# Fourier mixing and a two-layer MLP on one core: PSUM banks in a fixed turn, six output buffers, and a reordered first batch

## The chip, the cores and the metric

The kernel runs on one NeuronCore of a Trainium2 chip. The metric is the device time of one execution in microseconds. The engines are PE (matrix multiply), DVE (vector), ACT (scalar), POOL (GpSimd) and SP, which here only issues transfers. The span in a profile is about 1.8 us shorter than the time of the same execution. Full clock (warm) and half clock (cold) mean a granted PE clock of 1.00 and 0.50 in the trace; in the profile of the kernel before the inverse matmuls of 512 columns follow each other by 426 to 427 ns at 0.50 (33.3 to 34.6 us) and by 215 to 217 ns at 1.00 (35.0 to 36.3 us). In this kernel PE's results go into tiles of PSUM, one or two banks each; the program has another engine evacuate a tile (copy it, or multiply it into SBUF) before PE fills the bank again, and in the profile of before PE waits 2.51 us, to 32.09 us, for DVE to have done so.

## The reference, cut to what matters

Eight batches of 3008 positions x 256 channels are filtered along the sequence (real FFT, product with a complex filter, inverse FFT). The 24064 filtered rows then pass through a two-layer MLP, 256 to 2048 to 256, with a leaky ReLU between.

```python
X = np.fft.rfft(x, axis=1)
y = np.fft.irfft(X * (filt_r + 1j * filt_i)[None], n=x.shape[1], axis=1)
h = y.reshape(B * S, D) @ w_in
out = np.maximum(0.01 * h, h) @ w_out
```

## The kernel before

The FFT is factored as 94 x 32, so all of it is matmuls: a first stage (`s1`), a transpose on DVE (`t1`), a spectral stage (`s2`), the filter products, an inverse stage (`sa`), a second transpose (`t2`) and a last stage (`sb`). Batches 1 to 7 are interleaved with the MLP of earlier rows. Batch 0 has nothing to hide behind: it is done first, in two halves of 128 channels, by routines of its own (`first_s1`, `first_s2`, `first_sa`, `first_sb`). I call everything up to the first MLP matmul the head.

The filter products of the first batch are shared out. DVE takes the chunks that begin at frequency column 0 and 16, straight from PSUM. For chunks 8 and 20 ACT copies PSUM to SBUF (`fx`) and POOL multiplies. POOL's products are put into the pool of output buffers (`outp`), which is not yet needed for output.

```python
outp = ctx.enter_context(tc.tile_pool(name="outst", bufs=4))
php = ctx.enter_context(tc.tile_pool(name="php", bufs=2, space=bass.MemoryType.PSUM))   # two banks each
pop = ctx.enter_context(tc.tile_pool(name="pop", bufs=1, space=bass.MemoryType.PSUM))
pfp = ctx.enter_context(tc.tile_pool(name="pfp", bufs=3, space=bass.MemoryType.PSUM))
...
def first_s2(hf, c, n, on_pool):
    ps = php.tile([P, n, DH], FP32, tag="ph", name=f"f2_h{hf}_c{c}")
    ...                                     # spectral matmuls into ps
    if on_pool:
        y = [outp.tile([P, n, DH], FP16, tag="ost", name=f"fy{i}_h{hf}_c{c}") for i in range(2)]
        ...                                 # act copies ps to fx; gpsimd multiplies fx into y
    else:
        ...                                 # vector multiplies ps into y
...
first_s2(0, 8, 8, True)
first_s2(0, 0, 8, False)
first_s2(0, 20, 4, True)
first_s2(0, 16, 4, False)
for g in range(8):
    first_s1(1, g, two[0], dve if g in (1, 3, 6) else act)
x_load(1)
t1_part(0, 2, True)(), t1_part(0, 3, True)()
upper(1)
first_sa(0, 0), first_sa(0, 16)
first_s2(1, 8, 8, True)
nc.gpsimd.dma_start(w_out_sb[:], moe_w_out.rearrange("(ct p) d -> p ct d", p=P))
first_s2(1, 0, 8, False)
first_s2(1, 16, 8, False)
first_sa(0, 8), first_sa(0, 20)
first_sa(1, 0)
...                                         # t2, first_sa(1, 16), first_sa(1, 8), keep_warm, first_sb
```

Of the kernel before, what the change touches and what calls it, by code (L numbers as in the profile page):

```python
# [10 lines left out]
P = 128  # L11
FP16 = mybir.dt.float16
FP32 = mybir.dt.float32
AL = mybir.AluOpType
AF = mybir.ActivationFunctionType
# [3 lines left out]
N1, N2 = 94, 32  # L19
# [46 lines left out]
def kernel(  # L66
# [9 lines left out]
    nc = tc.nc  # L76
    B, N, D = x.shape
# [5 lines left out]
    CH = 512  # L83
# [21 lines left out]
    gtp = ctx.enter_context(tc.tile_pool(name="gtp", bufs=2))  # L105
    scrp = ctx.enter_context(tc.tile_pool(name="scr", bufs=2))
    ypp = ctx.enter_context(tc.tile_pool(name="ypp", bufs=4))
    outp = ctx.enter_context(tc.tile_pool(name="outst", bufs=4))
    php = ctx.enter_context(tc.tile_pool(name="php", bufs=2, space=bass.MemoryType.PSUM))
    pop = ctx.enter_context(tc.tile_pool(name="pop", bufs=1, space=bass.MemoryType.PSUM))  # L110
    pfp = ctx.enter_context(tc.tile_pool(name="pfp", bufs=3, space=bass.MemoryType.PSUM))


    po_ps = pop.tile([P, 2, D], FP32, name="po_ps")

    ctx.enter_context(tc.manual_schedule())

# [2 lines left out]
    DH = D // 2  # L120
# [36 lines left out]

    def s1_group(b, g, copy=nc.scalar.copy):
        def go():
            ps = pfp.tile([P, 2, D], FP32, tag="pf", name=f"s1_b{b}_g{g}")  # L160
            for j in range(2):
                n2 = 2 * g + j
                nc.tensor.matmul(ps[:, j, :], f1_sb[:N1, n2, :], x_sb[:N1, n2, :],  # L163
                                 start=True, stop=True)
            spread(big[(4 * b) % 3], 2 * g, ps, copy)
        return go


    def paired(t):
        return t[:].rearrange("p (e n t) -> p n e t", n=Q, t=2)  # L170

    def spread(dst, n0, ps, copy, e0=0):
        nn, de = ps.shape[1], ps.shape[2] // 2
        copy(paired(dst)[:, ds(n0, nn), ds(e0, de)], ps[:].rearrange("p n (e t) -> p n e t", t=2))  # L174

    E4 = D // 2 // 4

# [19 lines left out]
    ys = {}  # L197

    def s2_group(b, g):
        def go():  # L200
            ps = pfp.tile([P, 2, D], FP32, tag="pf", name=f"s2_b{b}_g{g}")
            src = big[(4 * b + 1) % 3][:].rearrange("p (n d) -> p n d", n=Q)
            nc.tensor.matmul(ps[:], fwd2, src[:, ds(2 * g, 2), :], start=True, stop=True)  # L203
            fa, fb = fa_sb[:, ds(2 * g, 2), :], fb_sb[:, ds(2 * g, 2), :]
            p1 = scrp.tile([P, 2, D], FP32, tag="p1", name=f"p1_b{b}_g{g}")
            p2 = scrp.tile([P, 2, D], FP32, tag="p2", name=f"p2_b{b}_g{g}")
            nc.vector.tensor_tensor(p1[:], ps[:], fa, AL.mult)  # L207
            nc.vector.tensor_tensor(p2[0:64], ps[64:P], fb[64:P], AL.mult)  # L208
            nc.vector.tensor_tensor(p2[64:P], ps[0:64], fb[0:64], AL.mult)  # L209
            y1 = ypp.tile([P, 2, D], FP16, tag="y", name=f"y_b{b}_g{g}")  # L210
            nc.gpsimd.tensor_tensor(y1[:], p1[:], p2[:], AL.add)  # L211
            ys[(b, g)] = y1
        return go

    def sa_group(b, g):
        def go():
            ps = pfp.tile([P, 2, D], FP32, tag="pf", name=f"sa_b{b}_g{g}")
            nc.tensor.matmul(ps[:], inv2, ys.pop((b, g))[:], start=True, stop=True)  # L218
            spread(big[(4 * b + 2) % 3], 2 * g, ps, nc.scalar.copy)
        return go  # L220

    def sb_group(b, g, copy, pool=(pfp, "pf")):
        dt, h = g // 8, g % 8

        def go():
            src = big[(4 * b + 3) % 3][:].rearrange("p (h n d) -> p h n d", h=2, n=Q)
            ps = pool[0].tile([P, 4, N1], FP32, tag=pool[1], name=f"sb_b{b}_g{g}")
            for j in range(4):
                n2 = 4 * h + j
                nc.tensor.matmul(ps[:, j, :], src[:, dt, n2, :], i1_sb[:, n2, :],  # L230
                                 start=True, stop=True)
            yv = yts[b % 2][:, dt, :].rearrange("p (a c) -> p a c", c=N2)
            copy(yv[:, :, ds(4 * h, 4)], ps[:].rearrange("p c a -> p a c"))  # L233
        return go


    two = ((pfp, "pf"), (php, "ph"))
    act, dve = nc.scalar.copy, nc.vector.tensor_copy

    def first_s1(hf, g, pool, copy):  # L240
        ps = pool[0].tile([P, 4, DH], FP32, tag=pool[1], name=f"f1_h{hf}_g{g}")
        for j in range(4):
            n2 = 4 * g + j
            nc.tensor.matmul(ps[:, j, :], f1_sb[:N1, n2, :], x_sb[:N1, n2, ts(hf, DH)],  # L244
                             start=True, stop=True)
        spread(big[0], 4 * g, ps, copy, hf * DH // 2)


    def first_s2(hf, c, n, on_pool):
        ps = php.tile([P, n, DH], FP32, tag="ph", name=f"f2_h{hf}_c{c}")  # L250
        src = paired(big[1])
        for j in range(0, n, 4):
            nc.tensor.matmul(ps[:, ds(j, 4), :].rearrange("p n (e t) -> p n e t", t=2), fwd2,
                             src[:, ds(c + j, 4), ts(hf, DH // 2)], start=True, stop=True)
        fs = [f[:, ds(c, n), ts(hf, DH)] for f in (fa_sb, fb_sb)]
        if on_pool:
            y = [outp.tile([P, n, DH], FP16, tag="ost", name=f"fy{i}_h{hf}_c{c}") for i in range(2)]
            xs = [scrp.tile([P, 4, DH], FP32, tag=f"p{j // 4 + 1}", name=f"fx_h{hf}_c{c + j}")
                  for j in range(0, n, 4)]
            for j, xf in enumerate(xs):  # L260
                act(xf[:], ps[:, ts(j, 4), :])
            for i in range(2):
                for j, xf in enumerate(xs):
                    nc.gpsimd.tensor_tensor(y[i][:, ts(j, 4), :], xf[:], fs[i][:, ts(j, 4), :], AL.mult)  # L264
        else:
            y = [ypp.tile([P, n, DH], FP16, tag=f"yw{i}", bufs=2, name=f"fy{i}_h{hf}_c{c}")
                 for i in range(2)]
            for i in range(2):
                nc.vector.tensor_tensor(y[i][:], ps[:], fs[i], AL.mult)  # L269
        ys[(hf, c)] = y  # L270

    def first_sa(hf, c):
        y = ys.pop((hf, c))
        for j in range(0, y[0].shape[1], 4):
            ps = pfp.tile([P, 4, DH], FP32, tag="pf", name=f"fa_h{hf}_c{c + j}")
            for i, m in enumerate((inv2, inv2x)):
                nc.tensor.matmul(ps[:], m, y[i][:, ds(j, 4), :], start=(i == 0), stop=(i == 1))
            act(paired(big[2])[:, ds(c + j, 4), ts(hf, DH // 2)],
                ps[:].rearrange("p n (t e) -> p n e t", t=2))


    def first_t2(i):
# [1 line left out]
        o = big[0][:].bitcast(FP32).rearrange("p (h n e r) -> p h e n r", h=2, n=Q // 2, r=2)  # L284
        nc.vector.transpose(o[:, i // 2, ts(i % 2, E4)], a)

    def first_sb(g, copy, pool):
        dt, h = g // 8, g % 8
        src = big[0][:].rearrange("p (h n e r t) -> p h n r t e", h=2, n=Q // 2, r=2, t=2)
        ps = pool[0].tile([P, 4, N1], FP32, tag=pool[1], name=f"fb_g{g}")  # L290
        for j in range(4):
            n2 = 4 * h + j
            for t in range(2):
                nc.tensor.matmul(ps[64 * t : 64 * t + 64, j, :], src[:, dt, n2 // 2, n2 % 2, t, :],  # L294
                                 i1_sb[:, n2, :], start=True, stop=True)
        yv = yts[0][:, dt, :].rearrange("p (a c) -> p a c", c=N2)
        copy(yv[:, :, ds(4 * h, 4)], ps[:].rearrange("p c a -> p a c"))

    def upper(hf):
        for t, cp in ((fa_sb, act), (fb_sb, dve)):  # L300
# [2 lines left out]

    def keep_warm(n):
        for _ in range(n):
            nc.tensor.matmul(po_ps[:].rearrange("p a d -> p (a d)"), small_sb[:, 0, :],
                             i1_sb[:].rearrange("p a d -> p (a d)")[:, 0:512],
                             start=True, stop=True)

# [6 lines left out]
    first_s2(0, 20, 4, True)  # L316
    first_s2(0, 16, 4, False)
    for g in range(8):
        first_s1(1, g, two[0], dve if g in (1, 3, 6) else act)
    x_load(1)  # L320
    t1_part(0, 2, True)(), t1_part(0, 3, True)()
    upper(1)
    first_sa(0, 0), first_sa(0, 16)
    first_s2(1, 8, 8, True)
    nc.gpsimd.dma_start(w_out_sb[:], moe_w_out.rearrange("(ct p) d -> p ct d", p=P))
    first_s2(1, 0, 8, False)
    first_s2(1, 16, 8, False)
    first_sa(0, 8), first_sa(0, 20)
    first_sa(1, 0)
    first_t2(0), first_t2(1)  # L330
    first_sa(1, 16), first_sa(1, 8)
# [13 lines left out]
    def moe1_group(ci, g):  # L345
        if g == 0:
            gts[ci] = gtp.tile([P, NCT, CH], FP16, tag="gt", name=f"gt_c{ci}")
        ph = php.tile([P, 2, CH], FP32, tag="ph", name=f"h_c{ci}_g{g}")
        pieces, t = [], ci * CH
        while t < (ci + 1) * CH:  # L350
            e = min((ci + 1) * CH, (t // N + 1) * N)
            pieces.append((t // N, t % N, t - ci * CH, e - t))
            t = e
        for j in range(2):
            ct = 2 * g + j
            for b, lo, o, ln in pieces:
                for dt in range(NDT):
# [2 lines left out]
                        yts[b % 2][:, dt, ds(lo, ln)],  # L360
                        start=(dt == 0), stop=(dt == NDT - 1),
                    )
        nc.scalar.activation(gts[ci][:, ds(2 * g, 2), :], ph[:], AF.Lrelu)  # L363

    def moe2_slice(ci, g):
        tj, half = g // 2, g % 2
        last = ci == NCHUNK - 1
        if last and half == 0:
            pos[ci] = pfp.tile([P, D], FP32, tag="pf", name=f"o_c{ci}_t{tj}")[:]
        po = pos[ci] if last else po_ps[:, tj % 2, :]  # L370
        for ct in range(8 * half, 8 * half + 8):
            nc.tensor.matmul(po, gts[ci][:, ct, ts(tj, P)], w_out_sb[:, ct, :],  # L372
# [77 lines left out]
```

## Time and profile before

| | before |
|---|---|
| time, median of the first 6 runs | 787.69 us (787.64 to 789.57) |
| span of the profiled run | 786.4 us |
| PE busy | 763.3 us, 97% |
| ACT, DVE, POOL busy | 556.9, 365.0, 150.6 us |
| first MLP matmul | 46.27 us |
| from there to the end | 740.03 us |

PE is busy for 97% of the span, so little can be gained; what there is lies in the first 46 us. The prediction shows the lines. Here, before and after, one line of the list of waits matters besides. It gives what PE waited for in total, how often, and the longest single wait; this is PE's wait for the two halves of the input of the first batch:

```profile
PE f_h_g L244 <- DMA x_sb<-in_x_dram: 9.5, 2, 9.2
```

### The profile page before, as it was taken

To read this page: it belongs to the slowest core of one execution; us is meant where nothing else is said; L and a number is where in the kernel's file an instruction comes from. 1 tells how busy PE (TensorE), PEld (TensorE's weight loads), DVE (VectorE), ACT (ScalarE), POOL (GpSimd) and SP (SyncE) were. 2 spreads that over 40 slices of the span, in tenths; PEclk is the share of its full clock that TensorE was granted. 3 is DMA by queue.
4 is the path that set the end of the run, shared out by engine and by line. 5 is a ranking of instruction groups with operands and counts; after the bars stand their busy time and mean duration, and the time that the engine had idled before them with its cause. 6 is when DMAs were issued, how large, how long until landed. Compare 5 with 4: busy or idle time off the path is not lost.

```text
span 786.4 us, 13584 instructions
## 1 busy us (share of the span) xinstructions
PE 763.3 (97%) x5812; PEld 527.9 (67%) x5812; DVE 365.0 (46%) x459; ACT 556.9 (71%) x794; POOL 150.6 (19%) x122
## 2 busy tenths in 40 slices
PE   3799999999999999999999999999999999999998
PEld 2356677666776677866777667776677667676666
DVE  4768760784327652386416764078432765200000
ACT  4686768676687767877687775967668776666664
POOL 6583400240003400042001410024000340000000
PEclk9999999999999999999999999999999999999999
DMA  9953010501032010501014101050100101101111
GB/s 176 203 68 95 28 42 28 121 28 41 28 76 73 28 41 28 117 33 42 28 41 108 40 29 41 28 119 28 43 28 28 41 28 42 41 28 41 41 41 54
DMA packets 42011, 43.38 MB, mean 55 GB/s; under 512 B 14274, under 2 KB 40514, under 8 KB 41282
## 3 DMA queue, kind: packets, MB, share of 16 engines
q0 software_dynamic: 15760, 16.99, 13.1%
q1 hardware_dynamic: 26192, 25.53, 9.3%
q8 instruction: 45, 0.74, 0.4%
q14 instruction: 14, 0.11, 0.0%
HBM read 34.10 MB, written 24.64 MB: 75 GB/s over the span
## 4 chain that ended last, share of the span: by engine, by line
PE 93%; ACT 3%; DVE 2%; DMA 1%; POOL 1%; issue 1%; POOLq 0%; ACTq 0%; DVEq 0%
PE po_ps L372 41%; PE h_c_g L358 40%; PE s_b_g L163 3%; PE sb_b_g L230 2%; PE s_b_g L203 2%; PE sa_b_g L218 2%; DMA x_sb<-in_x_dram 1%; DVE fy_h_c L269 1%; PE o_c_t L372 1%; ACT big L174 1%; ACT gt_c L363 1%; PE f_h_g L244 0%; POOL fy_h_c L264 0%; PE fb_g L294 0%; ACT fa_sb L301 0%
## 5 line engine op out<-in xcount | busy, mean ns | idle before, releaser
L363 ACT ACTIVATE gt_c<-h_c_g 128x1024 f16<-128x1024 f32 x376 | 384.6, 1023 | 194.0 <-PE h_c_g L358 193.0
L358 PE MATMUL h_c_g<-yt,w_in_sb 128*128 128x512 f16 (+7 forms) x1728 | 386.6, 352 | 0.7 <-ACT gt_c L363 0.4
L372 PE MATMUL po_ps<-w_out_sb,gt_c 128*128 128x256 f16 x2944 | 381.4, 273 | 0.6 <-ACT ost_c_t L379 0.6
L372 PEld LDWEIGHTS <-gt_c 128*128 128x128 f16 x3008 | 290.3, 98 | 87.1 <-issue 1.7
L358 PEld LDWEIGHTS <-w_in_sb 128*128 128x128 f16 x1728 | 162.7, 98 | 95.7 <-issue 1.4
L211 POOL TENSOR_TENSOR y_b_g<-p_b_g,p_b_g 128x512 f16<-128x512 f32 x84 | 106.9, 1273 | 225.7 <-DVE p_b_g L209 225.7
L186 DVE STREAM_TRANSPOSE big<-big 128x1024 f32<-128x1024 f32 x32 | 55.8, 1843 | 127.3 <-ACT big L174 127.1
L233 DVE CAST yt<-sb_b_g 128x376 f16<-128x376 f32 x112 | 56.3, 545 | 85.9 <-PE sb_b_g L230 85.9
L207 DVE TENSOR_TENSOR p_b_g<-s_b_g,fa_sb 128x512 f32<-128x512 f32 x84 | 58.1, 692 | 38.8 <-PE s_b_g L203 36.0
L379 ACT COPY ost_c_t<-po_ps 128x256 f32<-128x256 f32 x184 | 69.4, 377 | 7.4 <-PE po_ps L372 6.1
L194 DVE STREAM_TRANSPOSE big<-big 128x1024 f32<-128x1024 f32 x28 | 51.1, 1933 | 34.5 <-ACT big L174 34.5
L208 DVE TENSOR_TENSOR p_b_g<-s_b_g,fb_sb 64x512 f32<-64x512 f32 x84 | 58.2, 692 | 1.1
L209 DVE TENSOR_TENSOR p_b_g<-s_b_g,fb_sb 64x512 f32<-64x512 f32 x84 | 57.4, 683 | 1.1
L125 POOL DMA_DIRECT2D x_sb<-in_x_dram x12 | 8.5, 711 | 253.6 <-PE s_b_g L163 252.5
L174 ACT CAST big<-s_b_g 128x512 f16<-128x512 f32 x104 | 57.0, 607 | 0.0
L174 ACT CAST big<-sa_b_g 128x512 f16<-128x512 f32 x84 | 50.6, 602 | 0.0
L230 PEld LDWEIGHTS <-big 128*128 128x128 f16 x448 | 25.6, 98 | 13.2
L163 PE MATMUL s_b_g<-x_sb,f_sb 94*128 94x256 f16 x224 | 33.8, 272 | 0.3
L203 PE MATMUL s_b_g<-big,small_sb 128*128 128x512 f16 x84 | 31.9, 379 | 0.0
L218 PE MATMUL sa_b_g<-y_b_g,small_sb 128*128 128x512 f16 x84 | 31.9, 379 | 0.0
L230 PE MATMUL sb_b_g<-i_sb,big 128*128 128x94 f16 x448 | 28.7, 206 | 0.0
L163 PEld LDWEIGHTS <-f_sb 94*128 94x128 f16 x224 | 21.0, 97 | 9.1 <-issue 0.6
(42 smaller groups left out, 160.4 us busy)
## 6 DMA issues: line engine op xcount, KB each, us to landing
out_dram<-ost_c_t SPq DMA_DIRECT2D x92, 256.0 KB, 2.1
x_sb<-in_x_dram POOLq DMA_DIRECT2D x6, 1536.0 KB, 10.8
x_sb<-in_x_dram POOLq DMA_DIRECT2D x4, 384.0 KB, 10.2
w_in_sb<-in_moe_w_in_dram POOLq DMA_DIRECT2D x1, 1024.0 KB, 15.8
w_out_sb<-in_moe_w_out_dram POOLq DMA_DIRECT2D x1, 1024.0 KB, 9.9
x_sb<-in_x_dram POOLq DMA_DIRECT2D x1, 1024.0 KB, 9.1
f_sb<-fwd_const SPq DMA_DIRECT2D x4, 192.0 KB, 3.2
fa_sb<-in_filt_r_dram POOLq DMA_DIRECT2D x4, 192.0 KB, 10.0
```

Source lines behind the costliest of these rows:

```text
L163: nc.tensor.matmul(ps[:, j, :], f1_sb[:N1, n2, :], x_sb[:N1, n2, :], start=True, stop=True)
L174: copy(paired(dst)[:, ds(n0, nn), ds(e0, de)], ps[:].rearrange("p n (e t) -> p n e t", t=2))
L207: nc.vector.tensor_tensor(p1[:], ps[:], fa, AL.mult)
L208: nc.vector.tensor_tensor(p2[0:64], ps[64:P], fb[64:P], AL.mult)
L209: nc.vector.tensor_tensor(p2[64:P], ps[0:64], fb[0:64], AL.mult)
L211: nc.gpsimd.tensor_tensor(y1[:], p1[:], p2[:], AL.add)
L230: nc.tensor.matmul(ps[:, j, :], src[:, dt, n2, :], i1_sb[:, n2, :], start=True, stop=True)
L233: copy(yv[:, :, ds(4 * h, 4)], ps[:].rearrange("p c a -> p a c"))
L358: nc.tensor.matmul(ph[:, j, ds(o, ln)], w_in_sb[:, dt, ts(ct, P)], yts[b % 2][:, dt, ds(lo, ln)], start=(dt == 0), stop=(dt == NDT - 1),)
L363: nc.scalar.activation(gts[ci][:, ds(2 * g, 2), :], ph[:], AF.Lrelu)
L372: nc.tensor.matmul(po, gts[ci][:, ct, ts(tj, P)], w_out_sb[:, ct, :], start=(ct == 0), stop=(ct == NCT - 1))
L379: nc.scalar.copy(ost[:, tj % 2, :], po)
```

## The change

The intent is threefold: to let the kernel itself hand out PSUM banks in a fixed turn instead of a pool, to give POOL's products of the first batch buffers that nobody else is holding, and to spread the evacuations of the first batch's second half over five banks, with some reordering.

```diff
-    outp = ctx.enter_context(tc.tile_pool(name="outst", bufs=4))
-    php = ... bufs=2 ...; pop = ... bufs=1 ...; pfp = ... bufs=3 ...
+    outp = ctx.enter_context(tc.tile_pool(name="outst", bufs=6))
+    psp = ctx.enter_context(tc.tile_pool(name="psp", bufs=1, space=bass.MemoryType.PSUM))
+    wide = [psp.tile([P, 2 * CH], FP32, name=f"ph{i}") for i in range(2)]
+    single = [psp.tile([P, CH], FP32, name=f"pf{i}") for i in range(3)]
+    po_ps = psp.tile([P, 2, D], FP32, name="po_ps")
+    turn = {"ph": 0, "pf": 0}
+    def bank(kind, n, w):
+        of = wide if kind == "ph" else single
+        t = of[turn[kind] % len(of)]
+        turn[kind] += 1
+        return t[:, : n * w].rearrange("p (n w) -> p n w", n=n)
 ...   (every pool tile in PSUM becomes bank("pf", ...) or bank("ph", ...))
     for g in range(8):
-        first_s1(1, g, two[0], dve if g in (1, 3, 6) else act)
+        first_s1(1, g, two[g % 4 == 3], dve if g in (3, 5, 7) else act)
 ...
     first_s2(1, 8, 8, True)
+    first_s2(1, 0, 8, False)
     nc.gpsimd.dma_start(w_out_sb[:], ...)
-    first_s2(1, 0, 8, False)
+    first_sa(0, 8), first_sa(0, 20)
     first_s2(1, 16, 8, False)
-    first_sa(0, 8), first_sa(0, 20)
     first_sa(1, 0)
```

More of the change, by code (lines that the diff above doesn't have):

```diff
@@ L107 @@
     ypp = ctx.enter_context(tc.tile_pool(name="ypp", bufs=4))
-    outp = ctx.enter_context(tc.tile_pool(name="outst", bufs=4))
-    php = ctx.enter_context(tc.tile_pool(name="php", bufs=2, space=bass.MemoryType.PSUM))
-    pop = ctx.enter_context(tc.tile_pool(name="pop", bufs=1, space=bass.MemoryType.PSUM))
-    pfp = ctx.enter_context(tc.tile_pool(name="pfp", bufs=3, space=bass.MemoryType.PSUM))
-    po_ps = pop.tile([P, 2, D], FP32, name="po_ps")
+    outp = ctx.enter_context(tc.tile_pool(name="outst", bufs=6))
[9 more added lines that the diff above has]
+        return t[:, : n * w].rearrange("p (n w) -> p n w", n=n)
     ctx.enter_context(tc.manual_schedule())
@@ L159, in go @@
         def go():
-            ps = pfp.tile([P, 2, D], FP32, tag="pf", name=f"s1_b{b}_g{g}")
+            ps = bank("pf", 2, D)
             for j in range(2):
@@ L173, in spread @@
         nn, de = ps.shape[1], ps.shape[2] // 2
-        copy(paired(dst)[:, ds(n0, nn), ds(e0, de)], ps[:].rearrange("p n (e t) -> p n e t", t=2))
+        copy(paired(dst)[:, ds(n0, nn), ds(e0, de)], ps.rearrange("p n (e t) -> p n e t", t=2))
     E4 = D // 2 // 4
@@ L200, in go @@
         def go():
-            ps = pfp.tile([P, 2, D], FP32, tag="pf", name=f"s2_b{b}_g{g}")
+            ps = bank("pf", 2, D)
             src = big[(4 * b + 1) % 3][:].rearrange("p (n d) -> p n d", n=Q)
-            nc.tensor.matmul(ps[:], fwd2, src[:, ds(2 * g, 2), :], start=True, stop=True)
+            nc.tensor.matmul(ps, fwd2, src[:, ds(2 * g, 2), :], start=True, stop=True)
             fa, fb = fa_sb[:, ds(2 * g, 2), :], fb_sb[:, ds(2 * g, 2), :]
@@ L206, in go @@
             p2 = scrp.tile([P, 2, D], FP32, tag="p2", name=f"p2_b{b}_g{g}")
-            nc.vector.tensor_tensor(p1[:], ps[:], fa, AL.mult)
+            nc.vector.tensor_tensor(p1[:], ps, fa, AL.mult)
             nc.vector.tensor_tensor(p2[0:64], ps[64:P], fb[64:P], AL.mult)
@@ L216, in go, with sb_group @@
         def go():
-            ps = pfp.tile([P, 2, D], FP32, tag="pf", name=f"sa_b{b}_g{g}")
-            nc.tensor.matmul(ps[:], inv2, ys.pop((b, g))[:], start=True, stop=True)
+            ps = bank("pf", 2, D)
+            nc.tensor.matmul(ps, inv2, ys.pop((b, g))[:], start=True, stop=True)
             spread(big[(4 * b + 2) % 3], 2 * g, ps, nc.scalar.copy)
         return go
-    def sb_group(b, g, copy, pool=(pfp, "pf")):
+    def sb_group(b, g, copy):
         dt, h = g // 8, g % 8
@@ L226, in go @@
             src = big[(4 * b + 3) % 3][:].rearrange("p (h n d) -> p h n d", h=2, n=Q)
-            ps = pool[0].tile([P, 4, N1], FP32, tag=pool[1], name=f"sb_b{b}_g{g}")
+            ps = bank("pf", 4, N1)
             for j in range(4):
@@ L232, in go, with first_s1 @@
             yv = yts[b % 2][:, dt, :].rearrange("p (a c) -> p a c", c=N2)
-            copy(yv[:, :, ds(4 * h, 4)], ps[:].rearrange("p c a -> p a c"))
+            copy(yv[:, :, ds(4 * h, 4)], ps.rearrange("p c a -> p a c"))
         return go
-    two = ((pfp, "pf"), (php, "ph"))
+    two = ("pf", "ph")
     act, dve = nc.scalar.copy, nc.vector.tensor_copy
-    def first_s1(hf, g, pool, copy):
-        ps = pool[0].tile([P, 4, DH], FP32, tag=pool[1], name=f"f1_h{hf}_g{g}")
+    def first_s1(hf, g, kind, copy):
+        ps = bank(kind, 4, DH)
         for j in range(4):
@@ L249, in first_s2 @@
     def first_s2(hf, c, n, on_pool):
-        ps = php.tile([P, n, DH], FP32, tag="ph", name=f"f2_h{hf}_c{c}")
+        ps = bank("ph", n, DH)
         src = paired(big[1])
@@ L268, in first_s2 @@
             for i in range(2):
-                nc.vector.tensor_tensor(y[i][:], ps[:], fs[i], AL.mult)
+                nc.vector.tensor_tensor(y[i][:], ps, fs[i], AL.mult)
         ys[(hf, c)] = y
@@ L274, in first_sa @@
         for j in range(0, y[0].shape[1], 4):
-            ps = pfp.tile([P, 4, DH], FP32, tag="pf", name=f"fa_h{hf}_c{c + j}")
+            ps = bank("pf", 4, DH)
             for i, m in enumerate((inv2, inv2x)):
-                nc.tensor.matmul(ps[:], m, y[i][:, ds(j, 4), :], start=(i == 0), stop=(i == 1))
+                nc.tensor.matmul(ps, m, y[i][:, ds(j, 4), :], start=(i == 0), stop=(i == 1))
             act(paired(big[2])[:, ds(c + j, 4), ts(hf, DH // 2)],
-                ps[:].rearrange("p n (t e) -> p n e t", t=2))
+                ps.rearrange("p n (t e) -> p n e t", t=2))
     def first_t2(i):
@@ L285, in first_t2, with first_sb @@
         nc.vector.transpose(o[:, i // 2, ts(i % 2, E4)], a)
-    def first_sb(g, copy, pool):
+    def first_sb(g, copy, kind):
         dt, h = g // 8, g % 8
         src = big[0][:].rearrange("p (h n e r t) -> p h n r t e", h=2, n=Q // 2, r=2, t=2)
-        ps = pool[0].tile([P, 4, N1], FP32, tag=pool[1], name=f"fb_g{g}")
+        ps = bank(kind, 4, N1)
         for j in range(4):
@@ L296, in first_sb @@
         yv = yts[0][:, dt, :].rearrange("p (a c) -> p a c", c=N2)
-        copy(yv[:, :, ds(4 * h, 4)], ps[:].rearrange("p c a -> p a c"))
+        copy(yv[:, :, ds(4 * h, 4)], ps.rearrange("p c a -> p a c"))
     def upper(hf):
@@ L305, in keep_warm @@
         for _ in range(n):
-            nc.tensor.matmul(po_ps[:].rearrange("p a d -> p (a d)"), small_sb[:, 0, :],
+            nc.tensor.matmul(po_ps.rearrange("p a d -> p (a d)"), small_sb[:, 0, :],
                              i1_sb[:].rearrange("p a d -> p (a d)")[:, 0:512],
@@ L347, in moe1_group @@
             gts[ci] = gtp.tile([P, NCT, CH], FP16, tag="gt", name=f"gt_c{ci}")
-        ph = php.tile([P, 2, CH], FP32, tag="ph", name=f"h_c{ci}_g{g}")
+        ph = bank("ph", 2, CH)
         pieces, t = [], ci * CH
@@ L362, in moe1_group @@
                     )
-        nc.scalar.activation(gts[ci][:, ds(2 * g, 2), :], ph[:], AF.Lrelu)
+        nc.scalar.activation(gts[ci][:, ds(2 * g, 2), :], ph, AF.Lrelu)
     def moe2_slice(ci, g):
@@ L368, in moe2_slice @@
         if last and half == 0:
-            pos[ci] = pfp.tile([P, D], FP32, tag="pf", name=f"o_c{ci}_t{tj}")[:]
+            pos[ci] = bank("pf", 1, D)[:, 0, :]
         po = pos[ci] if last else po_ps[:, tj % 2, :]
```

## The prediction

Its sum comes to 787.69 - 2.4 = 785.3 us. The 2.4 us is the author's estimate between the 2.8 us worked out for a warm PE and the 1.75 us for a cold one.

> **What bounds the kernel now.** I read the busy times by stretch first, to see in which part of the 786.4 us a change of waits and buffers can matter at all.
>
> ```profile
> core 0: us, PE busy (x) PEld busy (x) DVE busy (x) ACT busy (x) POOL busy (x), PEclk, DMA share, GB/s
> ...
> 25.00:33.00 8.00, 5.02 (x13) 1.31 (x12) 5.68 (x5) 5.55 (x7) 0.60 (x2) 0.91 1.07 221
> 33.00:39.00 6.00, 5.10 (x18) 1.76 (x17) 4.73 (x4) 4.39 (x8) 4.45 (x4) 0.84 0.62 131
> ...
> 46.00:58.00 12.00, 11.08 (x65) 6.25 (x65) 7.34 (x11) 10.70 (x16) 10.66 (x2) 1.00 0.27 37
> 58.00:700.00 642.00, 641.45 (x4913) 447.82 (x4911) 330.86 (x420) 467.56 (x668) 110.09 (x90) 1.00 0.17 48
> ```
>
> From 58 us on PE is busy 641.45 of 642.00 us. Busy is not yet "at its peak", so I read the start times of the matmuls in the trace: after 60 us one 256-column matmul of the second MoE product follows another by 109 ns, one 512-column matmul follows another by 215 to 217 ns. That is about 0.42 ns per column everywhere: PE streams without a stop. Only the head, about 46 us up to the first MoE matmul, has time to give. (From 46 to 58 us ACT is the bound, 10.70 us of 12; the change leaves its work there as it is.)
>
> Next, the list of waits in the head, and its order of time (start, length, engine, line, tiles, count, idle before and what ended it):
>
> ```profile
> POOL fy_h_c L264 <- issue: 8.9, 1, 8.9
> ...
> PE f_h_c L253 <- DVE fy_h_c L269: 2.5, 1, 2.5
> ```
>
> ```profile
> 20.01 0.59 PE L253 MATMUL f_h_c<-big,small_sb 128*128 128x512 f16 x1 [0.67 <-ACT fx_h_c L261]
> ...
> 22.75 1.87 PE L244 MATMUL f_h_g<-x_sb,f_sb 94*128 94x128 f16 x16 [0.44 <-DVE big L174]
> ...
> 32.09 1.03 PE L253 MATMUL f_h_c<-big,small_sb 128*128 128x512 f16 x2 [2.51 <-DVE fy_h_c L269]
> 32.94 4.57 PE L277 MATMUL fa_h_c<-fy_h_c,small_sb 128*128 128x512 f16 x15
> 38.00 0.59 PE L277 MATMUL fa_h_c<-fy_h_c,small_sb 128*128 128x512 f16 x2 [0.49 <-POOL fy_h_c L264]
> 39.12 0.38 PE L277 MATMUL fa_h_c<-fy_h_c,small_sb 128*128 128x512 f16 x1 [0.52 <-POOL fy_h_c L264]
> 39.33 1.24 PE L306 MATMUL po_ps<-i_sb,small_sb 128*128 128x512 f16 x5
> 40.50 2.59 PE L294 MATMUL fb_g<-i_sb,big 128*64 128x94 f16 x64
> ```
>
> ```profile
> 29.48 1.11 ACT L261 COPY fx_h_c<-f_h_c 128x512 f32<-128x512 f32 x2
> ```
>
> ```profile
> 25.00 0.60 POOL L125 DMA_DIRECT2D x_sb<-in_x_dram  x1
> 34.55 2.28 POOL L264 TENSOR_TENSOR fy_h_c<-fx_h_c,fa_sb 128x512 f16<-128x512 f32 x2 [8.95 <-issue]
> 36.80 2.27 POOL L264 TENSOR_TENSOR fy_h_c<-fx_h_c,fb_sb 128x512 f16<-128x512 f32 x2
> ```
>
> POOL's four second-half products could read their input (fx, from ACT) at about 30.1 us but start at 34.55. The page calls that wait "issue"; the built program shows what it is: this instruction waits for PE. Its two outputs come from the pool of output buffers. There are four, all four hold the first half's products (chunks 8 and 20), and they come free only when PE has read chunk 8, in the run of 15 matmuls from 32.94 us. Those stand behind the chunk-16 matmul, held until 32.09 us for a PSUM bank that DVE was reading. So POOL ends at 39.08 us, and the chain of waits then goes from POOL 35.68 to 39.08, over the last inverse matmul 39.12, five warming matmuls 39.33, to the last stage at 40.50 and the MoE at 46.27 us. This is the path that sets the end.
>
> [...] 512-column matmuls follow each other by 427 ns up to 34.6 us and by 216 ns from 35.01 us on, and the granted clock is 0.50 in 31.6 to 34.9 us. [...] all ten POOL products took 1.15 us, and DVE's took 1.22 us beside them (18.55 us) and 1.23 us without (29.68 us).
>
> **The change part by part.**
>
> (a) *Banks in a fixed turn.* The instructions keep their number on each engine. What goes is 172 waits of PE for its own semaphore. They cost nothing: 127 first matmuls of an MoE group with such a wait start 109.3 ns after the matmul before, 87 without any wait 109.3 ns. 0 us. In the steady part the waits on other engines stay the same but for about a dozen in the batch-1 first stage (46 to 58 us), where ACT is busy anyway. 0 us.
>
> (b) *The fixed turn in the head.* Four spectral groups take the two wide banks in turn, chunks 8, 0, 20, 16. Before, chunk 16 took the bank that ACT had just emptied (20.01 us). In a fixed turn it gets chunk 0's bank and must wait for DVE: 19.69 + 1.21 = 20.90, so it starts near 20.95, 0.94 us later, and the second-half first stage behind it too.
>
> (c) *Second-half evacuations over five banks.* Groups 3 and 7 take wide banks, so the 0.44 us and other small gaps of PE around 22 us go. Eight groups of four matmuls at 107 ns: 21.38 + 8 x 0.43 = 24.8 us, where before they ended at 24.4. DVE's last evacuation ends near 25.7 and its two transposes (2.37) near 28.05 instead of 27.65. So (b) and (c) together lose about 0.4 us up to here.
>
> (d) *Six output buffers.* POOL no longer waits for PE. ACT's fx still ends at about 30.5 (first half 30.0): POOL runs 30.0 + 4 x 1.14 = 34.6 us, not 39.08. It is off the path then.
>
> (e) *Reordering.* First-half inverse matmuls of chunks 8 and 20 (six) move ahead of the chunk-16 spectral matmuls: they fill the 2.51 us in which PE waited. After the two spectral groups (28.1 + 4 x 0.43 = 29.8) they take 6 x 0.427 = 2.56 us cold, or 1.3 us warm.
>
> What sets the end then is DVE. Products of chunk 0 start at 30.0 (spectral matmuls at 28.9 + 1.06, the lag seen at 16.57 to 17.63) and end at 32.35. Warm: chunk 16 in PSUM at 32.15, DVE products to 34.7, inverse matmuls of chunks 16 and 8 (POOL's, ready 34.6) 34.75 + 8 x 0.216 = 36.5, warming 5 x 0.216 to 37.6, last stage from 37.7 instead of 40.50: 2.8 us gained. Cold: chunk 16 in PSUM at 33.4, DVE to 35.8, inverse 37.55, last stage 38.75: 1.75 us gained. DVE's last two transposes then end at 39.9 or 40.9 instead of 42.54, before the second half of the last stage needs them in both cases. [...] I weigh warm somewhat higher: 2.4 us. All behind it shifts along.
>
> Sum: 787.69 - 2.4 = 785.3 us, 0.3%.
>
> **Rivals.** *Only the wait moves* (POOL was late, but DVE's chain is nearly as long): for it speaks that DVE's chunk-16 products ended at 35.53 and only 36.07 to 38.44 and 40.16 to 42.54 follow; a cold PE would leave DVE later than before (35.8). It still frees POOL; a gain of 1 us or less, 786.9. *The fixed turn hurts in the steady part*: spectral results hold a bank for three DVE products, 3 x 0.69 = 2.07 us, and a strict turn of three might stall PE. Against it: the built programs have the same waits there. If each of 84 groups lost 0.1 us it would be 8 us more, 794. *The whole wait is saved*: 34.55 to 30.0 is 4.5 us, 783.2; against it, DVE's two product pairs and PE's matmuls lie in the way, as worked out above.
>
> **Range and chances.** Warm and cold span 784.9 to 786.0; the runs before spread from 787.64 to 789.57 us, and the head is hand-worked to some half a microsecond on either side: 784.1 to 787.1. Two per cent is 15.8 us, a third of the head; neither faster nor slower by that much is to be had from what moves. Faster 0.01, same 0.98, slower 0.01.
>
> **What would show it.** Right: POOL's second-half products start near 30 us with ACT as releaser; PE's 2.51 us wait is gone; chunk 16's first spectral matmul waits for DVE to 20.95; the chain passes through DVE's products instead of POOL; the first MoE matmul stands at 43.5 to 44.6 us instead of 46.27; from there to the end takes 740.1 us as before. Wrong: POOL still waits for PE, the first MoE matmul is at 46 us or later, or the part from it to the end changes by over 0.5 us, which would mean that the fixed turn acts in the steady part.

## The result and the profile after

The changed kernel took 785.47 us (median of 6 runs, 784.44 to 787.67) against 787.69 us. The ratio is 0.9971, with a 95% interval of 0.9953 to 0.9989. All ratios here are the mean time of one kernel's fast runs over that of the other's in the same rounds, so they are not quite the ratio of the medians quoted. At a threshold of 2% the two kernels count as the same; the gain of 0.3% is small, but its interval does not hold 1.

The profiled execution of the changed kernel is its slowest, 787.67 us. Its start explains part of that. The line of the list of waits that answers to the one shown of before is:

```profile
PE pf L251 <- DMA x_sb<-in_x_dram: 10.6, 2, 9.6
```

The input came 1.1 us later in this execution: PE starts on the second half of it at 12.45 us, where it was 11.35 us in the profile of the kernel before. Take 1.1 us off every time below to lay the two profiles over each other.

The head on PE, in order of time:

```profile
22.05 0.59 PE L260 MATMUL ph<-big,small_sb 128*128 128x512 f16 x1 [1.61 <-DVE fy_h_c L276]
...
29.31 1.88 PE L260 MATMUL ph<-big,small_sb 128*128 128x512 f16 x4 [1.33 <-DVE big L193]
31.02 2.74 PE L284 MATMUL pf<-fy_h_c,small_sb 128*128 128x512 f16 x6
33.55 1.05 PE L260 MATMUL ph<-big,small_sb 128*128 128x512 f16 x2
34.41 1.04 PE L284 MATMUL pf<-fy_h_c,small_sb 128*128 128x512 f16 x4
...
37.11 1.68 PE L284 MATMUL pf<-fy_h_c,small_sb 128*128 128x512 f16 x7 [0.74 <-DVE fy_h_c L276]
38.62 1.24 PE L313 MATMUL po_ps<-i_sb,small_sb 128*128 128x512 f16 x5
```

Three things are to be seen. The first chunk-16 spectral matmul now waits for DVE and starts at 22.05 us, which is 20.95 laid over the profile of before, where it was 20.01. The wait of 2.51 us ahead of the second-half chunk-16 matmuls is gone: the six inverse matmuls that were moved stand there (31.02), and the two spectral matmuls follow at 33.55 without a wait. The last inverse matmuls wait for DVE (37.11), no longer for POOL.

POOL's second-half products, in order of time:

```profile
31.21 2.26 POOL L271 TENSOR_TENSOR fy_h_c<-fx_h_c,fa_sb 128x512 f16<-128x512 f32 x2 [4.25 <-ACT fx_h_c L268]
```

They start at 31.21 us, 30.11 laid over the profile of before, with ACT as their releaser, instead of 34.55. And the chain that ended last (start, length, what) goes over DVE, not over POOL:

```profile
34.70 2.37 DVE fy_h_c L276 x2
37.07 0.04 issue
37.11 1.68 PE pf L284 x7
38.78 1.08 PE po_ps L313 x5
39.86 0.63 PE pf L301 x16
```

I split every profiled span in three, from start times in the trace: the landing (when PE starts on the second half of the input), the head from there to the first MLP matmul, and the tail from there to the end (taken 0.05 us before the span's end, in every run alike). Before they are 11.35 + 34.92 + 740.03 = 786.30 us; after, 12.45 + 33.11 + 740.27 = 785.83 us. So the head became 1.81 us shorter; the later landing gave back 1.10 of it and the tail 0.24.

One more thing had to be explained. The six times of the changed kernel are 784.44, 784.56, 784.71 and 786.23, 786.87, 787.67: they look like two groups.

### The profile page after: what moved, and what is told of

Read it like the earlier page. It is cut to its first block, busy times and chain, and to the rows that moved or that the text cites. A ratio compares the mean times of both kernels' runs of the same rounds, so it can differ in the third digit from the quotient of the medians.

```text
span 785.9 us, 13623 instructions
## 1 busy us (share of the span) xinstructions
PE 763.0 (97%) x5812; PEld 528.6 (67%) x5812; DVE 365.1 (46%) x459; ACT 557.0 (71%) x794; POOL 150.7 (19%) x122
## 4 chain that ended last, share of the span: by engine, by line
PE 93%; ACT 2%; issue 1%; DVE 0%; ACTq 0%; DVEq 0%
PE po_ps L379 41%; PE ph L365 40%; PE pf L170 3%; PE pf L237 2%; PE pf L210 2%; PE pf L225 2%; PE pf L379 1%; ACT big L181 1%; ACT gt_c L370 1%; PE pf L284 1%; PE ph L260 0%; PE ph L301 0%; DVE fy_h_c L276 0%; PE po_ps L313 0%; PE pf L301 0%
## 5 line engine op out<-in xcount | busy, mean ns | idle before, releaser
L370 ACT ACTIVATE gt_c<-ph 128x1024 f16<-128x1024 f32 x376 | 384.8, 1024 | 194.8 <-PE ph L365 193.8
L365 PE MATMUL ph<-yt,w_in_sb 128*128 128x512 f16 (+7 forms) x1728 | 386.6, 351 | 0.4 <-ACT yt L304 0.2
L181 ACT CAST big<-pf 128x512 f16<-128x512 f32 x195 | 111.8, 606 | 11.8 <-PE pf L251 11.7
L240 DVE CAST yt<-pf 128x376 f16<-128x376 f32 x112 | 56.3, 545 | 85.9 <-PE pf L237 85.9
L214 DVE TENSOR_TENSOR p_b_g<-pf,fa_sb 128x512 f32<-128x512 f32 x84 | 58.1, 692 | 38.0 <-PE pf L210 35.5
L215 DVE TENSOR_TENSOR p_b_g<-pf,fb_sb 64x512 f32<-64x512 f32 x84 | 58.2, 693 | 1.1
L216 DVE TENSOR_TENSOR p_b_g<-pf,fb_sb 64x512 f32<-64x512 f32 x84 | 57.4, 683 | 1.1
L170 PE MATMUL pf<-x_sb,f_sb 94*128 94x256 f16 x224 | 33.8, 272 | 0.1
L210 PE MATMUL pf<-big,small_sb 128*128 128x512 f16 x84 | 31.8, 379 | 0.0
L225 PE MATMUL pf<-y_b_g,small_sb 128*128 128x512 f16 x84 | 31.8, 379 | 0.0
L237 PE MATMUL pf<-i_sb,big 128*128 128x94 f16 x448 | 28.7, 206 | 0.0
```

What stands on the lines that cost most here:

```text
L170: nc.tensor.matmul(ps[:, j, :], f1_sb[:N1, n2, :], x_sb[:N1, n2, :], start=True, stop=True)
L181: copy(paired(dst)[:, ds(n0, nn), ds(e0, de)], ps.rearrange("p n (e t) -> p n e t", t=2))
L214: nc.vector.tensor_tensor(p1[:], ps, fa, AL.mult)
L215: nc.vector.tensor_tensor(p2[0:64], ps[64:P], fb[64:P], AL.mult)
L216: nc.vector.tensor_tensor(p2[64:P], ps[0:64], fb[0:64], AL.mult)
L237: nc.tensor.matmul(ps[:, j, :], src[:, dt, n2, :], i1_sb[:, n2, :], start=True, stop=True)
```

## The experiments

Each kernel below was profiled in one execution and timed five times (e5 and e11 six times) in rounds beside the kernel before, and all were correct. Runs 1 to 4, 5 to 8 and 9 to 12 each shared a chip and the runs of the kernel before, whose medians were 788.11, 788.09 and 787.65 us. "Six matmuls" in the table is the mean distance from one to the next of the six first-half inverse matmuls of chunks 8 and 20: 219 ns at full clock, 415 to 423 ns at half clock. Landing, head and tail are in us; they and the six matmuls come from start times in the traces.

| kernel | time (range) | ratio | landing | head | six matmuls, ns | tail |
|---|---|---|---|---|---|---|
| before | 787.69 (787.64 to 789.57) | | 11.35 | 34.92 | 415 | 740.03 |
| changed | 785.47 (784.44 to 787.67) | 0.9971 | 12.45 | 33.11 | 421 | 740.27 |
| e1 changed, again | 785.19 (784.53 to 786.15) | 0.9962 | 11.14 | 31.96 | 219 | 740.26 |
| e2 buffers only | 787.47 (786.92 to 788.48) | 0.9990 | 11.98 | 34.59 | 423 | 740.08 |
| e3 order only | 785.34 (785.13 to 786.02) | 0.9964 | 11.05 | 32.66 | 219 | 740.04 |
| e4 banks only | 787.81 (787.29 to 788.99) | 0.9995 | 11.91 | 33.59 | 219 | 740.50 |
| e5 chunk-16 bank | 785.10 (783.83 to 787.20) | 0.9965 | 12.74 | 32.18 | 421 | 740.46 |
| e6 four buffers | 786.35 (784.93 to 787.13) | 0.9978 | 10.93 | 33.11 | 421 | 740.23 |
| e7 warm | 784.63 (784.21 to 785.04) | 0.9959 | 11.07 | 31.88 | 219 | 740.24 |
| e8 warm, chunk-16 bank | 784.60 (783.85 to 785.39) | 0.9957 | 12.10 | 30.44 | 219 | 740.47 |
| e9 warm, four buffers | 784.67 (784.44 to 786.30) | 0.9962 | 12.37 | 31.88 | 219 | 740.23 |
| e10 warm, again | 784.57 (784.57 to 785.00) | 0.9959 | 10.89 | 32.05 | 219 | 740.23 |
| e11 warm, chunk-16 bank, again | 784.08 (783.32 to 785.33) | 0.9952 | 11.16 | 30.96 | 219 | 740.50 |
| e12 before, warm | 788.16 (786.74 to 788.93) | 0.9999 | 10.50 | 34.27 | 219 | 740.05 |

The landing differs by up to 2.2 us between executions (10.50 to 12.74) and hides differences in the head; that is why I read heads from the profiles as well as times.

### e1: the changed kernel again

No edit. The theory is that the clock makes the two groups. Expected:

> The changed kernel unaltered, for its spread. Its six times fell into two groups, 784.4 to 784.7 and 786.2 to 787.7 us. [...] The profiled run at 787.67 us had PE at full clock only in 27.2 to 30.6 us and then again from 34.0 us; a run near 784.5 us must show first-half inverse matmuls (six, behind the two spectral groups) at 216 ns instead of 427 ns, and its first MoE matmul near 43.5 us. Rival: the two groups come from when the input lands (second x transfer at 12.45 us there, 11.35 us in the kernel before): then the first MoE matmul minus that landing is the same 33.1 us in fast and slow runs, whatever the clock.

Measured: 785.19 us. The profiled execution was that of 785.19 us, and in it PE was at full clock. In the first changed run it was not; from the busy times by stretch of that run (the granted clock is the third column from the right, here 0.60 of full speed):

```profile
30.00:33.00 3.00, 3.00 (x8) 0.95 (x7) 1.96 (x3) 2.28 (x6) 1.79 (x2) 0.60 0.92 195
```

The six moved matmuls in e1, in order of time:

```profile
29.71 1.47 PE L284 MATMUL pf<-fy_h_c,small_sb 128*128 128x512 f16 x6
```

They take 1.47 us here and 2.74 us in the first run. The difference of the two executions is 787.67 - 785.19 = 2.48 us: 1.31 us of landing (12.45 - 11.14) and 1.15 us of head (33.11 - 31.96). So theory and rival are each about half of it. The two groups themselves did not come again: e1's five times fill the range between, so that there were two groups at all is not shown.

### e2: only the six buffers

```diff
-    outp = ctx.enter_context(tc.tile_pool(name="outst", bufs=4))
+    outp = ctx.enter_context(tc.tile_pool(name="outst", bufs=6))
```

> The kernel before with six output buffers and nothing else. Theory: POOL's second-half products start when ACT's copies are there, near 30.1 us, not 34.55; the wait of PE of 2.5 us near 32.1 us stays, for it is a PSUM bank. The last inverse matmuls are then held by DVE (35.53 us) and the run of PE: last stage near 39.2 us, a gain of 1.3 us, 786.4 us. Rival (buffers are all of it): 785.3 us, as the whole change. Rival (only the wait moves): 787.5 us.

Measured: 787.47 us, ratio 0.9990 with an interval that holds 1, and a head 0.33 us shorter. POOL did start early, on ACT:

```profile
30.83 2.26 POOL L264 TENSOR_TENSOR fy_h_c<-fx_h_c,fa_sb 128x512 f16<-128x512 f32 x2 [4.61 <-ACT fx_h_c L261]
```

But PE could not use it:

```profile
32.72 1.03 PE L253 MATMUL f_h_c<-big,small_sb 128*128 128x512 f16 x2 [2.51 <-DVE fy_h_c L269]
33.57 6.21 PE L277 MATMUL fa_h_c<-fy_h_c,small_sb 128*128 128x512 f16 x18
```

The bank wait of 2.51 us is still there, and behind it PE ran its inverse matmuls back to back, at half clock until 37.8 us. PE had become the bound. I expected 1.3 us. My working had the clock up at 35 us, as in the profile of before, so the buffers alone in an execution at full clock stay unmeasured. That six buffers are the whole gain is refuted.

### e3: only the order

```diff
     first_s2(1, 8, 8, True)
+    first_s2(1, 0, 8, False)
     nc.gpsimd.dma_start(w_out_sb[:], ...)
-    first_s2(1, 0, 8, False)
+    first_sa(0, 8), first_sa(0, 20)
     first_s2(1, 16, 8, False)
-    first_sa(0, 8), first_sa(0, 20)
```

> The kernel before with the new order alone (inverse matmuls of chunks 8 and 20 ahead of the chunk-16 spectral matmuls), four output buffers. Theory: the order frees POOL's buffers too, since PE reads chunk 8 right behind the spectral matmuls: POOL starts near 31.3 us. Chunk 16 still waits for DVE to 32.1 us in the old pools. Last stage near 38.8 us, a gain of 1.7 us, 786.0 us. Rival (the buffers are what matters): POOL not before 34 us, under 0.3 us gained, 787.5 us.

Measured: 785.34 us, ratio 0.9964, the same as the whole change (0.9962 beside it), and 2.8 us below the kernel before where I expected 1.7. With four buffers POOL starts at 30.07 us, earlier than the 31.3 expected:

```profile
30.07 2.27 POOL L264 TENSOR_TENSOR fy_h_c<-fx_h_c,fa_sb 128x512 f16<-128x512 f32 x2 [4.77 <-ACT fx_h_c L261]
```

The moved matmuls read chunk 8 early (29.10 to 29.98 us at full clock), so the two buffers come free before ACT has the input ready. PE still waits for DVE's bank at 31.79 us, as expected, but only for 1.21 us now that it has the six matmuls to do first:

```profile
31.79 1.02 PE L253 MATMUL f_h_c<-big,small_sb 128*128 128x512 f16 x2 [1.21 <-DVE fy_h_c L269]
```

Its head, 32.66, lies 0.7 us above the whole change's at full clock (31.96), but its tail is 0.22 shorter.

### e4: only the banks

The whole change with the edits of e2 and e3 and the assignment of the second-half evacuations taken back.

```diff
-    outp ... bufs=6
+    outp ... bufs=4
-        first_s1(1, g, two[g % 4 == 3], dve if g in (3, 5, 7) else act)
+        first_s1(1, g, two[0], dve if g in (1, 3, 6) else act)
     ...   (old order of first_s2 and first_sa)
```

> The fixed turn of banks alone: old order, four output buffers, second-half evacuations as before. Theory: two effects of opposite sign. The first chunk-16 spectral matmul starts near 20.95 us instead of 20.01 (it waits for DVE), and 0.8 us of that reaches the second half; but the second-half chunk-16 spectral matmuls get chunk 8's bank and no longer wait for DVE's products of chunk 0, so that the wait of 2.5 us goes and POOL starts near 33.5 us. Sum: a gain of some 0.9 us, 786.8 us. Rival (the turn only costs): 788.5 us.

Measured: 787.81 us, ratio 0.9995 with an interval that holds 1. The head of its profiled run was 1.33 us shorter than before's, and its tail 0.47 us longer. But its clock stood at full from 30.1 us on; against the kernel before at full clock (e12, head 34.27) its head is only 0.68 us shorter. Both effects of the theory show in start times, measured from the landing: the first chunk-16 matmul at 9.59 us (before: 8.66), the second-half one at 20.05 us (before: 20.74), held by ACT for 1.06 us and no longer by DVE's products for 2.51. POOL still waits for PE to read chunk 8:

```profile
31.96 1.02 PE L260 MATMUL ph<-big,small_sb 128*128 128x512 f16 x2 [1.06 <-ACT fx_h_c L268]
```

```profile
33.78 2.28 POOL L271 TENSOR_TENSOR fy_h_c<-fx_h_c,fa_sb 128x512 f16<-128x512 f32 x2 [6.93 <-PE pf L284]
```

Most of the 0.9 us that I expected is in the head of the profile and none is clear in the times; so the fixed turn alone gave no gain that the times show.

### e5: the other bank for the first chunk 16

The fixed turn gives chunk 16 the bank that DVE is still reading (PE waits 1.61 us for it, to 22.05 us, in the changed kernel). One step further in the turn gives it the bank that ACT has emptied.

```diff
+    turn["ph"] += 1
     first_s2(0, 16, 4, False)
```

> The changed kernel with the turn of the wide banks moved on by one before the first chunk-16 spectral matmul, so that it takes the bank that ACT has emptied, as before the change. Theory: it starts 0.9 us earlier against the chunk-0 products of DVE; the second-half first stage, transposes and all behind them come 0.5 to 0.9 us earlier: measured from the landing of the second x transfer, the first MoE matmul stands at 31.3 us with a warm PE (the changed kernel: 31.96), the time near 784.5 us. Rival: the evacuations by ACT and DVE bound that stretch, and nothing is gained: 785.2 us.

Measured: 785.10 us against 785.19 of the changed kernel (ratios 0.9965 and 0.9962): no gain in the times. Its profiled run fell on half clock and on the latest landing of all (12.74). The nearer neighbour is therefore the half-clock run of the changed kernel: head 32.18 against 33.11, 0.93 us shorter.

### e6: four buffers in the changed kernel

```diff
-    outp ... bufs=6
+    outp ... bufs=4
```

> The changed kernel with four output buffers again. Theory: the new order already frees them: POOL starts when PE has read chunk 8, some 0.7 us later than in the changed kernel (near 30.6 us), ends near 35.1 us, still before PE asks for its products (35.5 us): 785.2 us, the same as the changed kernel. Rival: the two extra buffers are needed, and about 1 us is lost: 786.2 us.

Measured: 786.35 us, ratio 0.9978: as the rival said, 1.2 us worse than e1, though the intervals touch (0.9966 to 0.9990 and 0.9949 to 0.9974). But its profiled head is 33.11 us at half clock, and the changed kernel's at half clock is 33.11 us too. The times leaned to "needed", the profiles said "no effect"; e9 tries it at full clock.

### e7: the clock held up

PE gets idle-time matmuls into the bank that the MLP's second product will use later. Nothing waits for them. Whether they hold the clock up is what the run tests. (The kernel itself does the same twice later, with `keep_warm`.)

```diff
+    def fill(n):
+        for _ in range(n):
+            nc.tensor.matmul(po_ps.rearrange("p a d -> p (a d)"), small_sb[:R1, 0, :],
+                             f1_sb[:].rearrange("p a d -> p (a d)")[:, 0:512], start=True, stop=True)
     for g in range(8):
         first_s1(0, g, two[(g // 2) % 2], (act, dve)[g % 2])
+    fill(7)
     ...
     first_sa(0, 0), first_sa(0, 16)
+    fill(3)
     first_s2(1, 8, 8, True)
```

> The changed kernel with ten idle-time matmuls into the unused bank: seven between the first-stage matmuls and the first spectral group, three before the second-half spectral group. They use nothing that the rest waits for. Theory (the clock makes the fast and slow runs): PE is at full clock all through the head from about 20 us on, the six first-half inverse matmuls always go at 216 ns, no run falls in the slow group, the median is 784.5 us and the time from the second x landing to the first MoE matmul is at most 31.96 us. Rival (the landing of the input makes the groups): the spread stays at some 1.5 us and the median at 785.2 us. Second rival: the filling matmuls overrun their gaps while cold and cost up to 1 us: 786 us.

Measured: 784.63 us; all five times lie in 784.21 to 785.04, and the six matmuls go at 219 ns. That part of the theory held. "At full clock from about 20 us on" did not: the clock came up at 25.75 us, only 1 us sooner than in e1. The first seven did not do what I meant them to do; the three in the gap before the second-half spectral group are the likelier cause, but the two were not run apart. The five profiled kernels with the filling and the changed order (e7 to e11) all show 219 ns; of the five with that order and no filling, three (changed, e5, e6) show 421 ns.

### e8: both

The edits of e5 and e7 together.

> Both: the filling matmuls and the chunk-16 bank of ACT. If both theories hold the gains add: first MoE matmul 31.0 us after the second x landing or earlier, 784.0 us. If the stretch is bound by the evacuations: as the warm version alone.

Measured: 784.60 us, as e7, although its profiled head is the shortest of all, 30.44 us, 1.44 below e7's. Its landing was 1.03 us later. And its clock was lucky: the trace grants it full speed from 18.82 to 22.24 us, and the first half of its second-half first stage went at 55 ns per matmul, where all other profiles show 107. So I ran the pair again.

### e9 to e12: the open points

e9 is e7 with `bufs=4`:

> The warm version (filling matmuls) with four output buffers. The changed kernel with four buffers took 786.35 us against 785.19, but its profiled run was one with PE at half clock in 29.5 to 32.9 us, and in it the first MoE matmul stood 33.11 us after the second x landing, the same as in the changed kernel's own half-clock run. Theory (the buffers do nothing once the order is new): with the clock held up, 31.9 us from landing to MoE and 784.6 us, as the warm version. Rival (the two buffers are worth 1 us): 785.6 us.

Measured: head 31.88 us, equal to e7's to the last digit, and 784.67 us against 784.57 of e10 beside it. POOL, now held by PE, starts 0.77 us later than in e7 measured from the landing:

```profile
31.82 2.27 POOL L271 TENSOR_TENSOR fy_h_c<-fx_h_c,fa_sb 128x512 f16<-128x512 f32 x2 [5.03 <-PE pf L284]
34.06 2.26 POOL L271 TENSOR_TENSOR fy_h_c<-fx_h_c,fb_sb 128x512 f16<-128x512 f32 x2
```

```profile
35.79 1.67 PE L284 MATMUL pf<-fy_h_c,small_sb 128*128 128x512 f16 x7 [0.74 <-DVE fy_h_c L276]
```

PE still does not wait for POOL: the last of the seven matmuls, which reads POOL's last product, starts at 37.08 us, and the product is done at 36.32. With the new order and the clock held up the two extra buffers do nothing. What made e6's times 1.2 us longer than e1's is not shown; clock and landing are the likelier causes. The profiled execution of e9 shows what a landing alone can do: it took 786.30 us at full clock, 1.26 us more than that of e7, and its landing was 1.30 us later.

e10 is e7 again:

> The warm version again, beside the next two on one chip: 784.6 us, 31.9 us from the second x landing to the first MoE matmul.

Measured: 784.57 us (784.57 to 785.00), head 32.05 us. As expected.

e11 is e8 again:

> The warm version with the chunk-16 bank of ACT again. In the profiles it was 1.4 us shorter from the second x landing to the first MoE matmul (30.44 against 31.88), in the times 784.60 against 784.63. Theory: the 1.4 us are real and the landing, which came 1 us later in its profiled run, hid them: 783.5 us here against 784.6. Rival: they are of that one execution (the clock fell well), and the two stay within 0.3 us.

Measured: 784.08 us with a head of 30.96 us, 1.09 below e10's. Over both pairs the mean of the eleven times with the chunk-16 bank is 784.35 us and that of the ten without 784.69 us: 0.34 us, where the heads of the profiles differ by 1.1 to 1.4 us and the tails give back 0.25. From the spread of these 21 times I estimate a 95% interval of about -0.1 to 0.8 us, so the gain in the times is not clear of noise. Neither theory nor rival fits well. Of the 1.44 us of the first pair, 0.52 is the difference between e8 and e11 (30.44 and 30.96), where e8 had the early full clock. What becomes of the rest stays open: an execution without a profile shows neither its landing nor its clock. This version has the lowest median measured, 3.6 us below the kernel before in the same rounds and some 1 us below the changed kernel in other rounds.

e12 is the kernel before with the filling matmuls of e7:

> The kernel before with the same filling matmuls. If the clock alone made the gain, it would reach 785.2 us too. Theory: the bank wait and the buffer wait remain; a full clock shortens the matmuls that POOL waits for (four from 32.94 us) by 0.8 us, so POOL starts near 33.7 us: 787.2 us, 0.8 us less than before.

Measured: 788.16 us, ratio 0.9999. The clock was up, the six matmuls went at 219 ns, and the head was 0.65 us shorter in the profile (expected: 0.8), but POOL still stood in its wait for a buffer:

```profile
33.05 2.28 POOL L264 TENSOR_TENSOR fy_h_c<-fx_h_c,fa_sb 128x512 f16<-128x512 f32 x2 [8.40 <-issue]
```

The times do not show the 0.65 us; landing and clock of the executions without a profile are not known. The clock alone does not make the gain; it only decides how much of it the new order brings (2.96 us of head at full clock, 1.81 at half, against the 34.92 us of before).

## Why the prediction was right or wrong

The prediction, 785.3 us in a range of 784.1 to 787.1, was right: 785.47 us measured. Of its signs, one needs care: the first MLP matmul of the profiled run stands at 45.56 us, outside the 43.5 to 44.6 named, and comes inside (44.46) only when the later landing of 1.1 us is taken off. Step by step:

- **Where time could be gained** held. The tail is 740.03 to 740.08 us in the four kernels with pools and 740.23 to 740.50 in the ten with the fixed turn. The steady part inside it, from the first to the last matmul of the second MLP product, is 723.82 to 723.84 us in all fourteen.
- **(a) The removed self-waits of PE** cost nothing, as the equal steady part shows. But "0 us" for the stretch from 46 to 58 us was wrong in size: from the first MLP matmul to the first of the second product it is 12.72 to 12.77 us with pools and 12.94 to 12.97 us with the fixed turn, 0.2 us lost. I had ACT "busy anyway" (10.70 of 12.00 us), but the stretch became longer all the same. In the traces 36 waits of ACT are for DVE where 8 were; that they are the cause is argued, not shown.
- **(b) The first chunk 16** was exact: 0.94 us later against the landing in e1 (9.60 against 8.66), and undoing it gives 0.93 us (e5), 1.44 (e8) and 1.09 (e11) of head back in the profiles, though not clearly in the times.
- **(c) The second half's transposes**: 0.4 us later was predicted, 0.5 measured (end of the second of them 16.81 us after the landing in e1, 16.30 before).
- **(d) Six output buffers** was wrong as an attribution. POOL did start at 30 us on ACT, but e3 has that with four buffers and e9 shows that two more change nothing. The new order alone frees them, because the read that POOL waited for moves ahead. I put the saving to the first cause that sufficed and did not ask whether another one sufficed too.
- **(e) The order** carries the gain: e3 alone gives 0.9964 against 0.9962. One thing is missing from that step: the fixed turn also gives the second-half chunk 16 another bank, so the wait for DVE would have gone without the filling (e4: 20.05 us after the landing instead of 20.74). The working used it silently ("in PSUM at 32.15") and named only its cost. The experiments show that two waits stood behind each other: e2 removes POOL's wait alone and e4 shortens PE's bank wait alone, neither gains in the times, and the order takes away the one and halves the other.
- **Warm and cold** were sized at 2.8 and 1.75 us of head. They measured 34.92 - 31.96 = 2.96 and 34.92 - 33.11 = 1.81 us. "I weigh warm somewhat higher" gave 2.4; the median says 2.2. That is partly luck: of the five profiles with the new order and no filling, in which PE's gap ahead of the second-half spectral matmuls was 0.92 to 1.46 us, three were cold. The "427 ns up to 34.6 us" was no proof of a cold PE either: the trace of before grants the full clock from 28.13 to 31.55 us, and the spectral matmuls in it go at 429 to 432 ns (see the last section). It did no harm, since the working counts them at 0.43 us warm and cold. The landing of the input, 10.50 to 12.74 us, was not in the working at all, though it moves single executions as much as the clock does. The range held all but the slowest of the six.
- **The rivals**: "only the wait moves" is what e2 shows for the buffers alone. "The fixed turn hurts in the steady part" fell with 723.84 us. "The whole wait is saved" fell: DVE's products and PE's matmuls stood in the way as predicted.

## What to carry to other kernels

When several parts of a change remove the same wait, each looks sufficient in a profile; only undoing them one at a time (e3, e9) tells which one is needed, and here moving six matmuls alone gave all the gain that the times show (0.9964 against 0.9962), where banks alone and buffers alone gave none. Banks and buffers together in the old order were not run. When the gain is 0.3% and lies in a head of 45 us, split each profiled span at an event such as the landing of the input, and compare heads at the same clock: the first run of the changed kernel and e6 differ by 0.9 us in the median and had the same head, 33.11 us. A fixed turn of banks is only as good as its order: look at which engine empties the bank that each user gets (here the first chunk 16 got DVE's instead of ACT's and started 0.94 us later).

## What the traces show of the clock, of strided operands and of the landing, and leave open

- The granted clock: in the traces of before and of the changed kernel its first two records last 3.41 us each (before: 1.00 from 28.13 us, 0.50 from 31.55; then 1.00 from 34.96). In the changed kernel it fell from 1.00 to 0.50 at 30.61 us, after 3.41 us with 56% of PE busy (27.20 to 30.61 us, 1.92 us busy by start times; the longest gap was 1.33 us). In e12 it stayed at 1.00 after 3.41 us with 55% (29.69 to 33.10 us, 1.87 us; counted in such steps from the rise at 26.28). Between these two busy time alone did not decide; what did is open.
- The spectral matmuls of the head read their moving operand in runs of two 2-byte elements and follow each other by 429 to 432 ns in the kernel before at a granted clock of 1.00 (28.1 to 29.0 us) and by 415 to 431 ns at 0.50 (32.1 to 32.9 us). The same 128x512 stage in the steady part, with a contiguous operand, goes at 216 ns at 1.00. So at a granted clock of 1.00 the matmuls with the strided operand went at half the rate here. No experiment changed the stride alone, so that the stride is the cause is not shown.
- The landing: PE started on the same transfer at 10.50 to 12.74 us in fourteen profiled executions, and POOL issued it at the same time in all (from 6.26 to 6.28 us on).
